# Preparing weights twice instead of storing them: a Strassen-type FNet and GEGLU kernel on one core

## The chip, the core and the metric

The kernel runs on one core of a Trainium2 chip. The metric is the device time of the whole program in microseconds (us). The engines are TensorE (PE: matmuls; PEld: its weight loads), VectorE (DVE), ScalarE (ACT), GpSimd (POOL) and SyncE (SP, which here only issues transfers).

## The reference

```
xn = layernorm(x)                                   # x: 2048 x 448
a, b = xn @ hid_re.T, xn @ hid_im.T
s = seq_re @ a - seq_im @ b                         # 2048 x 2048 matrices
g = silu((gelu(xn @ w_gate) * (xn @ w_up)) @ w_down) # 448 -> 1792 -> 448
out = x + s * g
```

## The kernel before

All matmuls take float32r operands, and a number is held as a high and a low part, so that one product of two blocks is three matmuls (`three`: high by high, high by low, low by high); a fourth, half-empty k-block is stacked so that it needs two (`two`). "Splitting" a tile is an ACT copy into the high part and a DVE subtract for the low part (`split`, L126).

The 2048 rows are four column tiles c = 0 to 3 of 512 (the columns of the transposed, normalised input: `xth`, `xtl`). The 1792 hidden features are 14 tiles f of 128. The tiles f = 0 and 1 are multiplied plainly. For f = 2 to 13 a block (`strassen`, L419) handles two columns c and e = c + 1 at once with seven-product sums of Strassen's kind. The second loop (L858) goes through these blocks twice: run p = 0 with columns 0 and 1, run p = 1 with columns 2 and 3, 24 blocks in all, numbered n. Everything is scheduled by hand: each engine does its instructions in the order of the program.

**A block.** PE makes x1, x2, x3, x4 in PSUM banks, later adds further products onto x1, x3 and x4, and where `q` is absent also makes an x5. ACT copies x1 to m; DVE forms u, m, c21 from the banks; ACT takes the gelu; DVE multiplies; the result is split into an `hs` tile (six of these in turn, `hs_tile`, L345). The second column's multiplication and split are left for the next block (`late`). Between the products PE does row tiles (`send`, `down_one`, L376): six matmuls of 448 columns that multiply hs by the prepared wd, added by DVE (for f = 0 and 1 copied by ACT) into `gacc`. Up to four are sent in a block, at dn[0] to dn[3]; their list dq grows by eight after every odd f. `preps` (before: one call, after the gelu of x1) holds the preparation of the next block's weights. DVE operations of the block in the profile: L443, L450, L455, L477, L478, L485, L491, L498, L503, and L394 for gacc.

**PSUM banks.** x1 to x5 take turns in banks 0 to 3 (`mm_tile`), row tiles in 6 and 7 (`o_tile`), and for later groups also in 4 and 5.

**Weights of a block.** `load_s` (L261) fetches ten raw 128x128 blocks of f into `raw` (512 KB at L265, 128 KB at L266). `sums_s` (L277) makes the Strassen sums in place, on POOL in the loop (L281 to L285). `split_s` (L287) then copies 15 blocks to the high part in one ACT operation (L290, 128x1920) and subtracts on DVE (L291, 128x1408; L292, 64x512 for the stacked blocks). The prepared weights lie in one of two slots; the slot of block n + 1 is filled during block n. In the first run they are also stored to device memory (`store_s`, L299: 960 KB and 704 KB), and in the second run they are fetched from there (`fetch_s`, L303), two blocks ahead, in three slots. The same is done with the prepared wd of a pair f, f + 1: `prep_d` (L318, ACT L320, DVE L321), stored at L834, fetched at L909.

**Terms of a run.** Besides the weights a block needs t1 to t4 (sums of the columns' k-blocks 0 and 1, `ts`) and, from some block on, q1 to q4 (the same with k-blocks 2 and 3, `tq`). They are made from the whole columns that lie in device memory as `xw`: transfers into tmp(0) and tmp(1), a DVE subtract, a split. In the first run q is made in `q_step` 0 to 3 (loads L673 to L683): step 0 before the blocks, 1 in f = 3, 2 and 3 in f = 4; q is used from f = 5. For the second run t is made in the last block of the first (`t1_load`, `t1_sums`, `t1_split`), q in its first block (`q_load1`, `q_step1`); q is used from its f = 3.

**Also on the queues.** `sum_step` (L745) copies and accumulates `sums` between places in device memory, used by the last stage: two copies of 896 KB on SP in one block out of three (L756), two accumulating ones on POOL two blocks later (L758). `gsp` keeps gacc of columns 2 and 3 during the first run, `sp` keeps column 1's xth and xtl, whose place holds q of the second run. At the end of the second run the hidden DFT matrices are loaded and split (`e_load`, `e_split`), and the next stage begins (`hid_mm`, L991), in which the last eight row tiles are sent, four behind each of its first two steps.

Of the kernel before, what the change touches and what calls it, by code (L numbers as in the profile page):

```python
# [8 lines left out]
F32 = mybir.dt.float32  # L9
# [4 lines left out]
P = 128  # L14
# [33 lines left out]
def fnet_geglu(ctx: ExitStack, tc: tile.TileContext, x, ca, ct, cp, et, wgu, wss, wd, out):  # L48
# [60 lines left out]
    turns = {"mm": 0, "tp": 0, "o": 0, "all": 0}  # L109

    def in_turn(kind, name):

        first, n = {"mm": (0, 4), "tp": (4, 2), "o": (6, 2), "all": (0, 8)}[kind]
        turns[kind] += 1
        return bank(first + turns[kind] % n, name)
# [152 lines left out]
    NAMES = ("s1", "s2", "s3", "s4", "s4q", "a11", "a12", "a22", "k2g", "k2u", "s2q")  # L268
# [8 lines left out]
    def sums_s(eng):  # L277


        r = raw_s.rearrange("p (b f) -> p b f", b=17)  # L280
        eng.tensor_add(r[:, 1:16:14], r[:, 0:14:13], r[:, 8:17:8])  # L281
        eng.tensor_sub(r[:, 3:15:11], r[:, 6:13:6], r[:, 0:14:13])
        eng.tensor_sub(r[:, 2], r[:, 1], r[:, 6])
        eng.tensor_sub(r[:64, 11], r[:64, 15], r[:64, 12])
        eng.tensor_sub(r[:, 4:6], r[:, 7:10:2], r[:, 2:12:9])  # L285

    def split_s(slot):  # L287
        h, l = slot
        src = raw_s[:, P:]
        nc.scalar.activation(h, src[:, :WH], AF.Copy)  # L290
        nc.vector.tensor_sub(l, src[:, :WL], h[:, :WL])  # L291
        nc.vector.tensor_sub(h[64:, WL:], src[64:, WL:WH], h[64:, WL:].bitcast(F32))  # L292
        return parts_of(slot)


    w_at = {f: dram.tile([P, WH + WL], F32, name=f"wp{f}") for f in range(2, NF)}
    d_at = {g: dram.tile([P, 4 * D], F32, name=f"dp{g}") for g in range(1, len(GROUPS))}

    def store_s(f, slot):  # L299
        nc.sync.dma_start(w_at[f][:, :WH], slot[0].bitcast(F32))  # L300
        nc.sync.dma_start(w_at[f][:, WH:], slot[1].bitcast(F32))

    def fetch_s(f, slot):  # L303
        nc.sync.dma_start(slot[0].bitcast(F32), w_at[f][:, :WH])
        nc.sync.dma_start(slot[1].bitcast(F32), w_at[f][:, WH:])
        return parts_of(slot)
# [11 lines left out]
    def prep_d(grp, rv, late=False):  # L318
        w = d_view(grp[0] // 2)
        nc.scalar.activation(w[:, 0], rv, AF.Copy)  # L320
        low = lambda: nc.vector.tensor_sub(w[:, 1], rv, w[:, 0])  # L321
        if late:
            return w, low
        low()
        return w
# [17 lines left out]
    hs_of, hs_n = {}, [0]  # L343

    def hs_tile():  # L345
        i = hs_n[0] % 6
        hs_n[0] += 1
        return a_h[i // 3][:, 1024 * (i % 3) :][:, :1024].rearrange("p (a b) -> p a b", a=2)

    def new_hs(f, c):  # L350
        hs_of[f, c] = hs_tile()
# [23 lines left out]

    def down_one(gi, c, wdn, kk):  # L376
        if gi > 0 and kk >= 2:
            po = tp_tile(f"po{gi}_{c}_{kk}")
        else:
            po = o_tile(f"po{gi}_{c}_{kk}")  # L380
        n = 0
        for i, f in enumerate(GROUPS[gi]):
            hs = hs_of[f, c]
            for a, b in ((0, 0), (0, 1), (1, 0)):
# [4 lines left out]
                n += 1  # L389
        ga = gacc[c][:, kk]  # L390
# [28 lines left out]
    def strassen(f, p, w, q, late, dn, preps):  # L419
# [8 lines left out]
        def bank(i):  # L428
            return mm_tile(f"x{i}_{f}_{p}")
# [3 lines left out]
        x1 = bank(1)  # L433
# [5 lines left out]
        x2 = bank(2)  # L439
# [6 lines left out]
        x3 = bank(3)  # L446
# [3 lines left out]
        nc.vector.tensor_add(m, u, x3)  # L450
        x4 = bank(4)
# [3 lines left out]
        nc.vector.tensor_add(m, m, x4)  # L455
# [6 lines left out]
        if f in GROUPS[1] and p == 0:  # L462
            preps()
            dn[1]()
        else:
            dn[1]()
            preps()
# [5 lines left out]
        if q:  # L473
            three(x3, w["k2u"], q[4])
        else:
            other(x3, w, 1, c)
# [31 lines left out]
    with tc.manual_schedule():  # L508
# [7 lines left out]
        junk = hs_tile()[:, 0]  # L516
# [98 lines left out]
        wdn, d_low = prep_d(GROUPS[0], draw, True)  # L615
# [52 lines left out]

        T = 1, 2, 4, 3

        def q_load(i):

            if i == 0:  # L673
                nc.sync.dma_start(tmp(0), xw_at(1, 3))
                nc.sync.dma_start(tmp(1), xw_at(0, 3))
            elif i == 1:
                nc.sync.dma_start(tmp(0), xw_at(1, 2))
            elif i == 2:
                nc.sync.dma_start(tmp(1), xw_at(0, 2))
            elif i == 3:  # L680
                nc.sync.dma_start(tmp(0), xw_at(1, 3))
                for r in range(2):
                    nc.sync.dma_start(tmp(1)[64 * r : 64 * r + 64], xw_at(1, 2)[:64])  # L683

        def q_step(i):
            if i == 0:
                tq[0] = eight(sb.tile([P, 4096], FR, name="tq0", tag="u1"))
            a, b = tmp(0), tmp(1)
            if i == 1:
                nc.vector.tensor_sub(a[:64], a[:64], b[:64])  # L690
            else:
                nc.vector.tensor_sub(b, *((a, b), None, (b, a), (b, a))[i])
            split(*tq[0][T[i]], a if i == 1 else b)
            q_load(i + 1)

        w_of = {}


        for c in (2, 3):
# [27 lines left out]
            else:  # L727
                t_split0(1)
                t_split0(2)
                nwdn, low_d = prep_d(GROUPS[1], draw, late=True)  # L730
                between1 = [lambda: t_split0(3), lambda: (t_split0(4), q_step(0))]
            m1, h1, l1 = gateup(1, c, ws[1], between1)
            m1()
            if c == 2:
                q_load(0)
                h1()
                l1()
                w_of[0, 2] = split_s(slots[0])
# [639 lines left out]
```

## Time and profile before

| what | value |
|---|---|
| time, median of three runs | 807.59 us (806.33 to 809.71) |
| profiled execution, its own time | 804.55 us |
| its span, first to last instruction | 802.8 us |
| matmuls | 4052 |
| mean granted TensorE clock | 0.989 |
| bytes moved by transfers | 205.95 MB |

In the views a row `A:B` is a stretch of the span in us: its length, then busy time and number of instructions of PE, PEld, DVE, ACT and POOL, the granted clock, the mean busy share of the 16 DMA engines, and GB/s. In a timeline a row has start, length, engine, line, operation, output and inputs, shapes and count, and in brackets the idle time of the engine before it with what ended it. In a group's row stand the count, the busy time, the mean ns of one, and after the bar the idle time ahead of it. In the list of transfers stand the issuing queue, the count, the size and the median us from issue to landing. In the chain a row has start, length and what the time went to.

### The profile page before, as it was taken

The page shows a single profiled execution, that of the slowest core. Times are in us where ns is not written, and L with a number is a line of the kernel's source. Part 1 is how long each engine was busy: PE and PEld are TensorE (multiplying, and loading weights), DVE is VectorE, ACT ScalarE, POOL GpSimd, SP SyncE. Part 2 cuts the span into 40 slices and gives each one's busy share as a digit, 9 for nine tenths or more (in the row PEclk, how much of TensorE's full clock was granted, in tenths as well). Part 3 has the DMA queues.
Part 4 walks back from the last instruction along what each step waited for, and adds up shares of the span by engine and source line. Part 5 has one row for each costly group of instructions (what it writes and reads, how often), then busy time and mean ns, then how long its engine had stood idle before and what let it go on. Part 6 is the DMA issues. An engine that isn't in the chain of part 4 may idle for free.

```text
span 802.8 us, 11336 instructions
## 1 busy us (share of the span) xinstructions
PE 774.4 (96%) x4052; PEld 691.3 (86%) x4052; DVE 598.2 (75%) x1045; ACT 316.2 (39%) x424; POOL 76.0 (9%) x102
## 2 busy tenths in 40 slices
PE   9999987999996899999999999999999999999997
PEld 7987776887875778888888999999999999999997
DVE  7877857768677575656576576789797977879697
ACT  3765333433233222212133475554444444444441
POOL 2002222412320000000000000000000000000000
PEclk9999998999999899999999999999999999999999
DMA  8476894999979999858852281396978979696985
GB/s 308 83 222 207 328 299 157 347 298 380 302 264 291 395 328 341 279 227 261 318 131 105 111 352 75 115 318 201 340 221 281 272 264 316 213 342 201 326 266 176
DMA packets 81928, 205.95 MB, mean 257 GB/s; under 512 B 8400, under 2 KB 58448, under 8 KB 80208
## 3 DMA queue, kind: packets, MB, share of 16 engines
q1 hardware_dynamic: 76256, 177.65, 61.4%
q0 software_dynamic: 5472, 27.46, 15.9%
q8 instruction: 32, 0.52, 0.3%
q14 instruction: 24, 0.20, 0.1%
q10 hardware_dynamic: 144, 0.11, 0.0%
HBM read 155.25 MB, written 79.30 MB: 292 GB/s over the span
## 4 chain that ended last, share of the span: by engine, by line
PE 79%; DMA 8%; DVE 6%; ACT 3%; POOL 2%; issue 2%; SPq 0%; DVEq 0%; POOLq 0%; ACTq 0%
PE p L1175 20%; PE x L405 16%; PE po L385 13%; PE p L1178 10%; PE ab L991 9%; PE x L417 3%; DMA w<-wp 3%; PE gu L335 2%; DMA raw<-wss 2%; PE py L1195 1%; PE py L1197 1%; PE py L1196 1%; DMA tmp<-xw 1%; ACT w L290 1%; PE gu L546 1%
## 5 line engine op out<-in xcount | busy, mean ns | idle before, releaser
L385 PE MATMUL po<-wd,hs 128*128 128x448 f32 x672 | 153.8, 367 | 1.8 <-ACT gacc L392 1.4
L385 PEld LDWEIGHTS po<-wd,hs 128*128 128x128 f32 x672 | 126.0, 188 | 17.8 <-ACT gacc L392 2.3
L405 PE MATMUL x<-xt,w 128*128 128x512 f32 x450 | 121.5, 395 | 10.7 <-DMA w<-wp 8.5
L405 PEld LDWEIGHTS x<-xt,w 128*128 128x128 f32 x450 | 85.0, 189 | 28.9 <-issue 8.4
L405 PE MATMUL x<-t,w 128*128 128x512 f32 x276 | 83.4, 404 | 8.3 <-DVE tmp L491 7.1
L394 DVE TENSOR_TENSOR gacc<-gacc,po 128x448 f32<-128x448 f32 x96 | 58.7, 616 | 36.0 <-PE po L385 35.8
L127 ACT ACTIVATE w<-raw 128x896 fp32r<-128x896 f32 (+1 forms) x60 | 54.6, 911 | 61.3 <-DVE raw L1081 31.6
L405 PEld LDWEIGHTS x<-t,w 128*128 128x128 f32 x276 | 53.1, 194 | 19.6 <-DVE tmp L491 7.9
L991 PE MATMUL ab<-w,xt 128*128 128x448 f32 x256 | 68.0, 365 | 0.0
L1175 PE MATMUL p<-xt,w 128*128 128x448 f32 x168 | 54.3, 374 | 0.0
L991 PEld LDWEIGHTS ab<-w,xt 128*128 128x128 f32 x256 | 48.1, 188 | 3.8
L480 ACT ACTIVATE hs<-tmp 128x512 fp32r<-128x512 f32 x24 | 15.2, 633 | 86.6 <-DVE tmp L478 86.6
L461 ACT ACTIVATE tmp<-x 128x512 f32<-128x512 f32 x24 | 14.4, 598 | 88.3 <-PE x L405 79.4
L127 ACT ACTIVATE w<-f 128x896 fp32r<-128x896 f32 (+1 forms) x34 | 30.2, 889 | 42.7 <-DVE f L1081 18.9
L128 DVE TENSOR_TENSOR w<-raw,w 128x896 fp32r<-128x896 f32 (+1 forms) x41 | 42.8, 1047 | 4.3 <-ACT w L127 3.8
L1220 POOL DMA_DIRECT2D cc<-x x14 | 12.4, 882 | 289.3 <-DVE raw L1080 107.4
L417 PE MATMUL x<-xt,w 128*128 128x512 f32 x116 | 37.0, 399 | 1.1 <-ACT xt L127 0.5
L1175 PE MATMUL p<-ts_g,w 128*128 128x448 f32 x112 | 36.4, 374 | 0.0
L1175 PE MATMUL p<-ts_u,ts_tmp 128*128 128x448 f32 x112 | 36.3, 374 | 0.0
L1175 PE MATMUL p<-hs,w 128*128 128x448 f32 x112 | 35.6, 374 | 0.0
L1080 DVE TENSOR_TENSOR raw<-raw 128x128 f32<-128x128 f32 x69 | 19.8, 287 | 20.8 <-DMA raw<-sums 20.4
L991 PE MATMUL ab<-wd,xt 128*128 128x448 f32 x96 | 35.1, 365 | 0.0
(273 smaller groups left out, 1700.5 us busy)
## 6 DMA issues: line engine op xcount, KB each, us to landing
sums<-ca SPq DMA_DIRECT2D x16, 896.0 KB, 11.0
sums<-ca POOLq DMA_DIRECT2D x16, 896.0 KB, 11.4
raw<-ct SPq DMA_DIRECT2D x69, 192.0 KB, 4.4
wp<-w SPq DMA_DIRECT2D x12, 960.0 KB, 7.3
w<-wp SPq DMA_DIRECT2D x12, 960.0 KB, 9.5
ts_u<-td SPq DMA_DIRECT2D x24, 448.0 KB, 6.0
ts_g<-td SPq DMA_DIRECT2D x24, 448.0 KB, 6.5
raw<-sums SPq DMA_DIRECT2D x69, 128.0 KB, 4.4
```

The source lines that it names most:

```text
L127: nc.scalar.activation(h, src, AF.Copy)
L128: nc.vector.tensor_sub(l, src, h)
L335: nc.tensor.matmul(ps[:, cols], a, xt[:, k, cols], start=n == 0, stop=n == len(mm) - 1)
L385: nc.tensor.matmul(po[:, :D], hs[:, a, kk * P : (kk + 1) * P], wdn[:, b, i], start=n == 0, stop=n == 5,)
L394: nc.vector.tensor_add(ga, ga, po[:, :D])
L405: nc.tensor.matmul(ps, a[i], b[j], start=first and n == 0, stop=n == 2, skip_group_check=True)
L417: nc.tensor.matmul(ps, a[0], x_, start=False, stop=True, skip_group_check=True)
L480: nc.scalar.activation(hs[:, 0], g1, AF.Copy)
L991: nc.tensor.matmul(p[:, :D], a, b, start=n == 0, stop=n == len(mm) - 1)
L1080: nc.vector.tensor_add(s2, cr1, s1)
L1175: nc.tensor.matmul(ps[q][:, :D], h, v, start=u % UN == 0, stop=False, skip_group_check=True)
L1178: nc.tensor.matmul(ps[q][:, :HD], l, v[:, :HD], start=False, stop=u % UN == NS - 1, skip_group_check=True,)
```

## The change

- **Weights prepared anew.** `store_s`, `fetch_s` and the two stores in device memory (`wp`, `dp`) are removed. Blocks of both runs load the raw weights, sum them on POOL and split them; the wd of each pair is loaded and split in both runs. Slots alternate by n; the last block has a third slot.
- **Preparation dealt out.** The order of the raw blocks is changed so that the seven plain ones lie together. `split_s` gives three parts, and a block has three places for them: the plain blocks ahead of x3, then POOL's sums; the high parts of the sums after x4; the low parts where preparation stood, followed by the next raw load.
- **The terms, one step a block.** `t_load` and `t_step` replace the routines for q and t: subtract, high and low part at the three places, the low part followed by the loads of the next step. First run: q in f = 2, 3 and 4 (step 0's subtract before them, the rest of it and step 1 in f = 2); t of the second run in f = 6 to 9; its q in f = 10, 11, 12 and in the second run's f = 2. `sp` is stored at f = 9 instead of 8.
- **Banks.** x1 to x4 have banks 0 to 3, x5 has 2, and the product that was added onto x3 has a bank of its own, 4 (x6). Row tiles take turns in 5, 6 and 7.
- **Row tiles a step later.** In f = 2 two are sent and in f = 3 two (before one and three), in f = 4 three, and in the second run's f = 12 six instead of five; in the next stage three behind each of the first three steps. An hs tile is given back to a list when its last row tile is sent.
- **DFT matrices.** One is split in f = 12 and three in f = 13, instead of two and two.

```diff
-    turns = {"mm": 0, "tp": 0, "o": 0, "all": 0}
+    turns = {"mm": 0, "tp": 0, "o": 0, "x": 0, "po": 0, "all": 0}
...
     def split_s(slot):
...
-        nc.scalar.activation(h, src[:, :WH], AF.Copy)
-        nc.vector.tensor_sub(l, src[:, :WL], h[:, :WL])
-        nc.vector.tensor_sub(h[64:, WL:], src[64:, WL:WH], h[64:, WL:].bitcast(F32))
-        return parts_of(slot)
+        n = 6 * P
+        def plain():
+            nc.scalar.activation(h[:, n : n + 7 * P], src[:, n : n + 7 * P], AF.Copy)
+            nc.vector.tensor_sub(l[:, n:], src[:, n:WL], h[:, n:WL])
+        def high():
+            nc.scalar.activation(h[:, :n], src[:, :n], AF.Copy)
+            nc.scalar.activation(h[:, WH - 2 * P :], src[:, WH - 2 * P : WH], AF.Copy)
+        def low():
+            nc.vector.tensor_sub(l[:, :n], src[:, :n], h[:, :n])
+            nc.vector.tensor_sub(h[64:, WL:], src[64:, WL:WH], h[64:, WL:].bitcast(F32))
+        return plain, high, low
-    def store_s(f, slot):
-    def fetch_s(f, slot):
...
     def strassen(f, p, w, q, late, dn, preps):
+        def x_tile(i):
+            return bank((0, 1, 2, 3, 2, 4)[i - 1], f"x{i}_{f}_{p}")
...
         dn[0]()
+        preps[0]()
-        x3 = bank(3)
+        x3 = x_tile(3)
         three(x3, w["s3"], t3, True)
...
-        nc.vector.tensor_add(m, u, x3)
+        nc.vector.tensor_add(c21, u, x3)
...
-        nc.vector.tensor_add(m, m, x4)
+        nc.vector.tensor_add(m, c21, x4)
+        preps[1]()
...
             dn[1]()
-            preps()
+            preps[2]()
+        x6 = x_tile(6)
+        three(x6, w["a22"], t4, True)
...
         if not q:
-            x5 = bank(5)
+            x5 = x_tile(5)
             other(x5, w, 1, e, True)
-            nc.vector.tensor_add(m, m, x5)
-        three(x3, w["a22"], t4)
...
-        nc.vector.tensor_add(c21, u, x3)
+        nc.vector.tensor_add(c21, c21, x6)
         nc.vector.tensor_mul(g1, g1, c21)
...
+        if not q:
+            nc.vector.tensor_add(m, m, x5)
...
+        def t_load(i, p, k1, k2):
+            c, e = 2 * p, 2 * p + 1
+            for n, v in ({0: (e, k1), 1: (c, k1)}, {0: (e, k2)}, {1: (c, k2)}, {0: (e, k1)}, {})[i].items():
+                nc.sync.dma_start(tmp(n), xw_at(*v))
...
+        def t_step(i, places, p, k1, k2):
...
+            return sub, high, low
...
+        def weights(n):
+            if n == len(blocks):
+                return [], [], []
+            slot = slots[2 if n == len(blocks) - 1 else n % 2]
+            w_of[blocks[n]] = parts_of(slot)
+            plain, high, low = split_s(slot)
+            next_ = [lambda: load_s(blocks[n + 1][1])] if n + 1 < len(blocks) else []
+            return [plain, lambda: sums_s(nc.gpsimd)], [high], [low, *next_]
...
+        for n, (p, f) in enumerate(blocks):
             g = f // 2
             dn, q = [send] * 4, tq[p]
+            prep = weights(n + 1)
+            step = []
+            if f % 2 == 0 and n:
+                d_raw[0] = load_d(GROUPS[g])
+            if f % 2 and 1 < n < len(blocks) - 1 or n == len(blocks) - 2:
+                prep[1].append(lambda: weights_d(g))
+                prep[2].append(lambda: low_of[g]())
             if p == 0:
                 if f == 2:
+                    prep[0][:0] = q_steps[0][1:]
+                    prep[2].append(q_steps[1][0])
+                    dn = [nop, send, q_steps[1][1], then(send, q_steps[1][2])]
                     nc.sync.dma_start(gsp[0], gacc[2].rearrange("p k d -> p (k d)"))
                 elif f == 3:
+                    dn = [nop, send, send, low_d]
                 elif f == 4:
+                    dn[0] = nop
...
+                if 2 < f < 5:
+                    step = [q_steps[f - 1]]
+                elif 6 <= f < 12:
+                    step = [t1_steps[f - 6]]
+                elif f == 12:
+                    step = [t1_steps[6][:1]]
+                if f == 9:
                     nc.sync.dma_start(sp, a_x[1].bitcast(F32))
+            elif f == 2:
+                q = None
+                for v, w in zip(prep, (*t1_steps[6][1:], t1_steps[7][0])):
+                    v.append(w)
+                dn[2:] = [then(send, v) for v in t1_steps[7][1:]]
...
+            elif f == NF - 3:
+                e_load(2)
+            elif f == NF - 2:
+                dn[1] = dn[3] = then(send, send)
+                prep[2].append(lambda: e_split(2))
+                prep[2].extend([lambda b=b: e_load(b) for b in (1, 0, 3)])
+            elif f == NF - 1:
+                prep[2].extend([lambda b=b: e_split(b) for b in (1, 0, 3)])
+                dn = [then(send, send), send, nop, nop]
+            if step:
+                for v, w in zip(prep, step[0]):
+                    v.append(w)
+            prep = [then(*v) for v in prep]
             late = strassen(f, p, w_of[p, f], q, late, dn, prep)
...
+            elif p == 0 and f == 5:
+                t_load(0, 1, 0, 1)
+            elif p == 0 and f == 9:
+                t_load(0, 1, 3, 2)
             sum_step(n)
...
-            if k < 2:
-                for _ in range(4):
+            if k < 3:
+                for _ in range(3):
                     send()
```

More of the change, by code (lines that the diff above doesn't have):

```diff
@@ L374, in gateup @@
         return act(f, c, pg)
+    sends = [False]
     def down_one(gi, c, wdn, kk):
[L377 to L380, printed above, removed]
+        po = in_turn("po" if sends[0] else "o", f"po{gi}_{c}_{kk}")
         n = 0
@@ L389, in down_one @@
                 n += 1
+        if kk == 3:
+            hs_free.extend(hs_at.pop((f, c)) for f in GROUPS[gi])
         ga = gacc[c][:, kk]
@@ L438, in strassen @@
         late[0]()
-        x2 = bank(2)
+        x2 = x_tile(2)
         three(x2, w["s2"], t2, True)
@@ L871, in fnet_geglu @@
                 elif f == 4:
+                    dn[0] = nop
+                if f < 5:
                     q = None
[L873 to L882 removed]
```

236 lines of the change are left out of this document (75 added, 161 removed).

## The prediction

> **What bounds the kernel now.** I read the page first, for the shares and the chain of work that ended last.
>
> ```profile
> span 802.8 us, 11336 instructions
> PE 774.4 (96%) x4052; PEld 691.3 (86%) x4052; DVE 598.2 (75%) x1045; ACT 316.2 (39%) x424; POOL 76.0 (9%) x102
> PE 79%; DMA 8%; DVE 6%; ACT 3%; POOL 2%; issue 2%; SPq 0%; DVEq 0%; POOLq 0%; ACTq 0%
> ```
>
> PE is the bound, and the change leaves it the same matmuls. So nothing can be won but time in which PE waits or runs at a lower clock. A tenth of the chain, DMA and POOL, is not PE's. To find where, I cut the part that the change touches (72.19 to 431.85 us) at the starts of the blocks, as PE's timeline shows them. The two runs through the columns have twelve blocks each, f = 2 to 13; the first row below is f = 2 of the first run, the tenth is f = 2 of the second.
>
> ```profile
> core 0: us, PE busy (x) PEld busy (x) DVE busy (x) ACT busy (x) POOL busy (x), PEclk, DMA share, GB/s
> 72.19:84.49 12.30, 11.11 (x48) 8.66 (x47) 8.90 (x12) 4.96 (x7) 2.40 (x3) 1.00 0.61 237
> 84.49:99.06 14.57, 13.56 (x60) 10.92 (x59) 11.85 (x16) 5.82 (x8) 4.08 (x5) 1.00 0.99 360
> 99.06:114.03 14.97, 14.54 (x66) 12.12 (x65) 11.27 (x17) 6.07 (x9) 5.55 (x7) 1.00 1.03 334
> 114.03:137.46 23.43, 16.37 (x64) 13.48 (x63) 13.29 (x19) 6.15 (x8) 4.07 (x5) 0.85 0.53 157
> 137.46:178.78 41.32, 41.32 (x190) 35.49 (x189) 30.52 (x45) 14.99 (x19) 11.81 (x17) 1.00 0.96 317
> 178.78:208.70 29.92, 28.71 (x127) 23.35 (x126) 25.27 (x36) 10.32 (x13) 8.55 (x12) 1.00 1.00 371
> 208.70:222.48 13.78, 13.78 (x64) 11.64 (x62) 6.76 (x11) 4.00 (x6) 3.01 (x5) 1.00 0.87 255
> 222.48:240.47 17.99, 16.15 (x64) 12.99 (x64) 15.52 (x21) 6.32 (x8) 3.92 (x5) 0.91 0.76 284
> 240.47:254.24 13.77, 13.77 (x64) 11.64 (x62) 11.02 (x18) 5.09 (x8) 1.65 (x2) 1.00 1.03 281
> 254.24:279.09 24.85, 16.32 (x67) 13.30 (x67) 15.05 (x26) 5.75 (x10) 0.00 (x0) 0.86 1.02 371
> 279.09:294.13 15.04, 14.33 (x64) 11.75 (x63) 11.88 (x20) 4.51 (x9) 1.64 (x2) 1.00 1.02 364
> 294.13:431.85 137.72, 137.72 (x632) 118.30 (x630) 84.19 (x132) 32.66 (x54) 4.93 (x6) 1.00 0.74 242
> ```
>
> The last row is ten blocks with PE busy throughout, so an undisturbed block takes 13.77 us. It holds 39 products of 512 columns and four row tiles (24 matmuls of 448). Next, what PE waited for where a block took longer.
>
> ```profile
> 74.75 2.07 PE L405 MATMUL x<-t,w 128*128 128x512 f32 x6 [1.05 <-ACT tmp L360]
> 97.74 1.49 PE L385 MATMUL po<-wd,hs 128*128 128x448 f32 x6 [0.96 <-ACT gacc L392]
> 124.98 1.65 PE L405 MATMUL x<-t,w 128*128 128x512 f32 x3 [7.06 <-DVE tmp L491]
> 223.33 0.73 PE L405 MATMUL x<-xt,w 128*128 128x512 f32 x2 [0.69 <-ACT w L290]
> 224.99 0.50 PE L405 MATMUL x<-xt,w 128*128 128x512 f32 x1 [0.93 <-DVE w L291]
> 228.00 1.32 PE L405 MATMUL x<-tq,w 128*128 128x512 f32 x3
> 229.16 1.40 PE L385 MATMUL po<-wd,hs 128*128 128x448 f32 x6
> 262.47 1.19 PE L405 MATMUL x<-xt,w 128*128 128x512 f32 x2 [8.06 <-DMA w<-wp]
> 421.82 2.60 PE L385 MATMUL po<-wd,hs 128*128 128x448 f32 x12
> 424.25 0.86 PE L405 MATMUL x<-t,w 128*128 128x512 f32 x3
> ```
>
> Twelve row-tile matmuls take 424.25 - 421.82 = 2.43 us, 0.2025 each, a row tile 1.215; so a product takes (13.77 - 24 x 0.2025) / 39 = 0.2285. The fourth view, the chain in order of time, says what stood behind the waits.
>
> ```profile
> 110.19 10.91 DMA tmp<-xw
> ...
> 207.73 10.45 DMA raw<-wss
> ...
> 240.88 23.21 DMA w<-wp
> ```
>
> All three are transfers that landed late and were issued in stretches whose DMA share stood near 1. The wait at 124.98 is named after DVE, but DVE itself was standing behind the first of these, the rows for q_step(3). The one at 262.47 is the fetch of the stored weights for the second run's first block.
>
> **What can be had.** Blocks f = 2, 3, 4 of the first run and f = 2 of the second have 41 products instead of 39 (0.46 more), and the first run's f = 2 and 3 send one and three row tiles instead of four. Ideal and lost, in us: f2 13.77 + 0.46 - 3.65 = 10.58, lost 1.72; f3 13.01, lost 1.56; f4 14.23, lost 0.74; f5 9.66; f6 to f8 nothing; f9 and f10 2.38; f11 nothing; f12 4.22; f13 nothing; second run f2 24.85 - 14.23 = 10.62; f3 1.27; the rest nothing. The sum is 32.2 us: 20.3 in the first run, 11.9 in the second. The row tiles are only dealt out differently (43 and 49 instead of 44 and 48 before the next stage), so the ideal stays. No edit can win more than this in these blocks, and the change touches the later stage only in how eight remaining row tiles are spread.
>
> **The change part by part.** First the transfers.
>
> ```profile
> wp<-w SPq DMA_DIRECT2D x12, 960.0 KB, 7.3
> w<-wp SPq DMA_DIRECT2D x12, 960.0 KB, 9.5
> raw<-wss SPq DMA_DIRECT2D x12, 512.0 KB, 5.7
> ...
> DMA to landing us min/median/max: 3.4/5.7/10.7
> ```
>
> The last line is for the 512 KB loads of raw weights (L265). Storing the prepared weights (960 KB and 704 KB a block) and fetching them again goes, as do the stores and fetches of the prepared wd (896 KB a pair of blocks). By the sizes in the code the first run moves 640 (raw) + 1664 + 224 + 448 + 1195 (four sums of 896 KB in three blocks) = 4171 KB a block now, which is the 317 GB/s and 0.96 share of the row from 137.46. After, it is 640 + 224 + 1195 and up to 512 for the row tiles of t1 and q: 2570 KB at most, a share near 0.6. The second run goes from 1664 + 448 + 1195 = 3307 to about 2060 KB.
>
> So the fetch ahead of the second run (10.6 us lost) has nothing in its place: its first block's weights are prepared in the block before, as all others. The raw loads that were late in f9, f10 and f12 (2.4 + 4.2) have less in front of them. The rows for q's last step are asked for in f3 and used in f4, a good half block later, no longer within f4; of f5's 9.7 most should go. The two waits for gacc copies in f3 and f4 came from two banks; now three take turns, and the 1920-wide ACT copy is in three pieces.
>
> What is added to the engines: twelve more preparations, in the second run. Prices:
>
> ```profile
> L291 DVE TENSOR_TENSOR w<-raw,w 128x1408 fp32r<-128x1408 f32 x11 | 17.9, 1625 | 19.5 <-ACT w L290 19.5
> L292 DVE TENSOR_TENSOR w<-raw,w 64x512 fp32r<-64x512 f32 x11 | 7.6, 690 | 0.3
> L321 DVE TENSOR_TENSOR wd<-raw,wd 128x896 fp32r<-128x896 f32 x6 | 6.5, 1090 | 0.1
> L128 DVE TENSOR_TENSOR tq<-tmp,tq 128x512 fp32r<-128x512 f32 x4 | 3.0, 761 | 2.8 <-ACT tq L127 2.8
> L498 DVE TENSOR_TENSOR tmp<-tmp 128x512 f32<-128x512 f32 x11 | 8.5, 773 | 2.2 <-ACT tmp L494 2.2
> ...
> L498 DVE TENSOR_TENSOR tmp<-tmp 128x512 f32<-128x512 f32 x8 | 5.5, 686 | 0.0
> L290 ACT ACTIVATE w<-raw 128x1920 fp32r<-128x1920 f32 x7 | 12.6, 1805 | 9.7 <-POOL raw L285 9.7
> ```
>
> DVE does (84.19 - 2 x 1.09) / 10 = 8.2 us a block in the second run (the two are splits for the next stage). Weights add 1.63 + 0.69 and about 0.16 for cutting one subtract in two (an estimate: between 64x512 and 128x1408 a column costs 1.04 ns, which leaves 0.16 fixed): 10.7, and 11.8 where a wd is prepared. In the first run f6 to f11 take t1's and q's steps on top, a subtract and a split of 0.69 to 0.76: 12.2, and 13.3 with a wd. All stay under 13.77, the last by only 0.5. ACT's extra 1.8 and a wd copy every second block, and POOL's 3.0 (row from 208.70), are far from a limit. So DVE still hides behind PE, though a heavy block makes it some 2.5 us late: it stands idle until the second row tile, then has the low parts, the wd and the step ahead of its next PSUM read. PE bears that: bank 4 is wanted a block later, and the sum that frees x4 is done before this queue. If that cover goes, PE pays the excess.
>
> PSUM: the last gate-up pair lies in banks 1 and 2, so x2 of f2 waits for the gelu on bank 1 as x3 does now; ACT is freer there since q's first split moved behind. Between nothing and the 1.05 of now: I take 0.8. A separate bank for x6 takes the place of adding onto x3 and costs no DVE operation: three before and three after.
>
> New waits on in-order engines: DVE and ACT now stand behind row tiles of xw in f2 to f4; behind them on DVE are the sum that frees bank 2 for x5 and the one that frees x4. The cost lies between a gain and the 9.66 of f5; a transfer asked for half a block ahead at a share of 0.6 is nearer to none: 1.2. In the second run's f2, step 7 waits for rows asked for behind 1.8 MB of gacc, and x3 of f3 needs its result: between 0 and the 10.62 of now, nearest to the 1.27 that the same place cost in f3: 0.8. Three splits for the next stage instead of two fall in the last block, the last one after the next stage has begun: 0 to 1.09, I take 0.5. Late weights elsewhere: 0.2. Together 3.5.
>
> On SP's queue the two stores stood between a raw load and the sums of that block. They are gone, but the row-tile loads stand there instead, each waiting for DVE's low part of a step, and the sums wait behind them; in f2 this sends the first sums some 3 us later. POOL's accumulations wait for those sums and for the new sums_s ahead of them on POOL; the sums are used in the last stage only, so this costs nothing unless they block a raw load, which the third rival prices.
>
> How much such remnants cost depends on the clock. In f12 the waits were 0.69 + 0.93 and a few tenths, but the block lost 4.22, since PE ran at (229.16 - 228.00) / 3 = 0.39 us a product for some time after. By that row 3.5 us of waits could cost 8. The Trainium skill (TensorE: Matmul & The Clock Gate, Part 1) has the clock halve after an idle window of about 3.4 us; by that rule waits this short cost only themselves and the sum stays. f12 speaks against it, so both ends are kept.
>
> **Sum.** The profiled execution took 804.55 us, 1.75 more than its span, against a median of 807.59 (806.33 to 809.71) of three runs, 1.0038 of it. 804.55 - 32.2 + 3.5 = 775.9; on the scale of the median 778.8 us.
>
> **Rivals.** *The waits move along.* The in-order DVE and ACT stand behind the row tiles as long as PE did: f5's 9.66 returns in full, and half of the second run's 10.62, less the 2.0 counted: 775.9 + 13.0 = 788.9, 792 by the median. For it: q's last rows have 1.8 MB of sums and a weight load ahead of them. Against: the share.
>
> *DVE and POOL exclude each other.* L498 takes 773 ns in the first run, where POOL works, and 686 in the second. If a sum on POOL held DVE for its whole length, 3.0 us would be added to a block: in f6 to f11 12.75 + 3.0 - 13.77 = 2.0, twelve in all, and in the second run 11.25 + 3.0 - 13.77 = 0.5, six: 794 us, 797 by the median. Against: in f6 to f8 POOL works and PE loses nothing. The Trainium skill (SBUF — State Buffer, Who interferes with whom) states such an exclusive lock for a DVE operation with two SBUF inputs; the 87 ns show it as occasional.
>
> *Slower: the raw load becomes a chain through all blocks.* It is issued when DVE has the low parts, about 11 us into a block; the next block's ACT copy, DVE subtract, the sums behind it and then x4's second half (11.1 us in) hang on it with about 3.5 us of work, as do POOL's sums and the next weights. So it must land within about 10.3 us; each us beyond is lost in 22 blocks. It decides at 10.3, and is slower than before from 11.8. At 12.5: 776 + 48 = 824, 827 by the median. For it: 10.7 was seen, and 10.45 in the chain. Against: the median of 5.7, under a heavier load.
>
> **How the numbers follow.** Forecast 0.73, moved waits 0.13, exclusion 0.04, slower chain 0.05, and 0.05 that something unseen eats the gain (0.04 to no change, 0.01 to slower). About 0.5% (4 us) is what a measurement of this kernel can tell from no change. Faster 0.90; same 0.04; slower 0.06. The range starts at 773, the ideal by the median (775.3) less the spread of runs, and ends at 793, with the doubled remnants (784) and the first rival in it.
>
> **What would show it.** Right: no w<-wp or dp rows, PE busy all through 254 to 270, blocks of 13.77 us, DVE about 11 us a block in the second run, the part from 72 us to the next stage near 331 us instead of 359.7. Wrong: PE waiting for DVE w or ACT w in many blocks (third rival); blocks of 14 to 16 us with DVE full (second); a PE gap of several us in f3 to f5, or in f2 and f3 of the second run, with DVE behind tmp<-xw (first).

## The result, and the profile after

The changed kernel takes 778.82 us (median of six runs, 776.04 to 780.49) against 807.70 us (six runs, 806.33 to 809.71). The ratio is 0.9636, with a 95% interval of 0.9611 to 0.9661. The forecast was 778.8.

The profiled execution of the changed kernel is the longest of its six: 780.49 us, with a span of 778.7. From its page, the busy time of the engines, the transfers, and the chain by engine:

```profile
span 778.7 us, 11499 instructions
...
PE 766.2 (98%) x4052; PEld 687.8 (88%) x4052; DVE 639.2 (82%) x1099; ACT 347.1 (45%) x490; POOL 126.4 (16%) x162
...
DMA packets 80634, 165.46 MB, mean 212 GB/s; under 512 B 8000, under 2 KB 62656, under 8 KB 78912
...
PE 61%; DVE 15%; DMA 14%; issue 3%; ACT 3%; POOL 2%; SPq 1%; DVEq 0%; POOLq 0%
```

PE does the same 4052 matmuls and is now busy for 98% of the span instead of 96%. DVE has 41 us more to do and POOL 50 us more; 40.5 MB fewer are moved. That the chain's share of PE fell from 79% to 61% says little, I think: once nearly every block is full, a chain traced backwards can run through work that ended just in time.

The same part as before, cut at the starts of the blocks. The first four rows are f = 2 to 5 of the first run, the fifth is f = 6 to 10, then f11, f12 and f13; the ninth and tenth are f = 2 and 3 of the second run, then its other ten blocks, and the last row is the next stage.

```profile
core 0: us, PE busy (x) PEld busy (x) DVE busy (x) ACT busy (x) POOL busy (x), PEclk, DMA share, GB/s
72.14:84.44 12.30, 12.03 (x54) 9.87 (x53) 11.03 (x16) 6.21 (x11) 3.42 (x6) 1.00 0.41 99
84.44:96.22 11.78, 11.78 (x54) 9.95 (x53) 11.31 (x16) 6.51 (x12) 3.55 (x4) 1.00 0.56 210
96.22:109.22 13.00, 13.00 (x60) 11.07 (x59) 12.63 (x18) 5.33 (x9) 6.96 (x7) 1.00 0.84 224
109.22:123.00 13.78, 13.78 (x65) 11.83 (x63) 9.92 (x15) 5.24 (x9) 3.59 (x5) 1.00 0.43 109
123.00:191.86 68.86, 68.86 (x316) 59.15 (x315) 63.61 (x94) 28.83 (x47) 23.38 (x29) 1.00 0.70 214
191.86:209.46 17.60, 14.21 (x64) 11.56 (x62) 11.07 (x17) 6.33 (x10) 3.41 (x5) 1.00 0.56 138
209.46:223.46 14.00, 14.00 (x63) 11.86 (x64) 13.29 (x20) 4.75 (x8) 3.68 (x5) 1.00 0.67 229
223.46:237.24 13.78, 13.78 (x65) 11.83 (x64) 12.97 (x19) 5.70 (x9) 5.52 (x7) 1.00 0.55 117
237.24:252.16 14.92, 14.49 (x66) 12.12 (x65) 10.33 (x17) 5.50 (x9) 3.93 (x5) 1.00 0.91 293
252.16:267.60 15.44, 14.05 (x64) 11.75 (x63) 14.97 (x22) 6.11 (x10) 3.77 (x5) 1.00 0.51 176
267.60:406.53 138.93, 138.93 (x637) 119.44 (x636) 113.73 (x167) 55.45 (x87) 41.11 (x53) 1.00 0.60 165
406.53:778.70 372.17, 367.16 (x2161) 345.40 (x2159) 297.62 (x551) 169.56 (x198) 14.54 (x18) 1.00 0.73 242
```

Read it by the lengths: f = 5 to 10 and f13 are at 13.77 to 13.78 us, and f = 3 and 4 at their own ideal (11.8 and 13.0 for fewer row tiles). Five blocks are not: f2 (0.5 over its ideal of 11.80), f11 (3.8), f12 (0.2), and f2 and f3 of the second run (0.7 and 1.7), 6.9 us in all where there were 32.2. The granted clock is 1.00 in every row. The part from 72 us to the next stage took 406.53 - 72.14 = 334.4 us instead of 359.7 (near 331 was foretold). The next stage took 372.17, 1.2 more than before (370.95).

PE's timeline at the waits that are left:

```profile
73.93 1.66 PE L403 MATMUL x<-t,w 128*128 128x512 f32 x6 [0.27 <-DVE tmp L359]
...
205.61 1.66 PE L403 MATMUL x<-xt,w 128*128 128x512 f32 x6 [2.40 <-DVE tmp L454]
...
209.46 0.98 PE L403 MATMUL x<-xt,w 128*128 128x512 f32 x3 [0.99 <-ACT tmp L461]
...
246.66 0.96 PE L403 MATMUL x<-xt,w 128*128 128x512 f32 x3 [0.43 <-DVE tmp L449]
...
258.37 0.51 PE L415 MATMUL x<-xt,w 128*128 128x512 f32 x1 [1.39 <-DVE xt L701]
...
407.78 0.67 PE L984 MATMUL ab<-w,xt 128*128 128x448 f32 x2 [0.48 <-DVE w L845]
```

The largest, at 205.61 in f11, is named after DVE. As with the waits of the kernel before, one has to follow it back: the timelines of POOL, SP, ACT and DVE in that stretch.

```profile
187.79 1.66 POOL L776 DMA_DIRECT2D sums<-ca  x2
...
190.47 0.33 SPq L265 DMA_DIRECT2D raw<-wss  x1
...
200.44 0.95 ACT L294 ACTIVATE w<-raw 128x896 fp32r<-128x896 f32 x1 [3.84 <-DMA raw<-wss]
...
201.43 0.83 DVE L295 TENSOR_TENSOR w<-raw,w 128x640 fp32r<-128x640 f32 x1 [3.56 <-ACT w L294]
...
203.39 0.77 DVE L690 TENSOR_TENSOR tmp<-tmp 64x512 f32<-64x512 f32 x1 [1.14 <-DMA tmp<-xw]
...
204.87 0.69 DVE L454 TENSOR_TENSOR tmp<-tmp,x 128x512 f32<-128x512 f32 x1
```

POOL issues the two accumulating transfers of 896 KB at 187.79, SP asks for the raw weights at 190.47, and they are there only at about 200.4: some 10 us. ACT, DVE, the rows for a step of q (`tmp<-xw`) and the sum that frees x4 are late one after the other. The window of that load, and the landing times of all 512 KB loads in this kernel:

```profile
190.47:200.42 9.95, 9.95 (x47) 8.57 (x46) 6.85 (x11) 2.39 (x4) 0.00 (x0) 1.00 0.99 227
```

```profile
DMA to landing us min/median/max: 3.3/3.7/10.0
```

While the load was on its way the mean share of the DMA engines was 0.99. Over the loop this is a pattern. Seven raw loads are asked for while a pair of accumulations is under way, and they take 7.4 to 10.0 us; six of them land 0.2 to 0.7 us behind the pair's second transfer. The others of the loop take 3.3 to 3.8 us, but for one of 6.9 behind the 2 MB store of `sp`.

### The profile page after: what moved, and what is told of

It is laid out like the page before. It is cut to its first block, busy times and chain, and to the rows that moved or that the text cites. A ratio compares the mean times of both kernels' runs of the same rounds, so it can differ in the third digit from the quotient of the medians.

```text
span 778.7 us, 11499 instructions
## 1 busy us (share of the span) xinstructions
PE 766.2 (98%) x4052; PEld 687.8 (88%) x4052; DVE 639.2 (82%) x1099; ACT 347.1 (45%) x490; POOL 126.4 (16%) x162
## 4 chain that ended last, share of the span: by engine, by line
PE 61%; DVE 15%; DMA 14%; issue 3%; ACT 3%; POOL 2%; SPq 1%; DVEq 0%; POOLq 0%
PE p L1168 14%; PE x L403 11%; PE po L381 10%; PE ab L984 9%; PE p L1171 7%; DMA raw<-wss 5%; DMA raw<-sums 4%; PE gu L330 3%; PE x L415 2%; DMA out<-cc 1%; DVE w L128 1%; PE gu L548 1%; DVE w L302 1%; PE py L1188 1%; PE py L1190 1%
## 5 line engine op out<-in xcount | busy, mean ns | idle before, releaser
L403 PE MATMUL x<-xt,w 128*128 128x512 f32 x450 | 119.7, 392 | 3.8 <-DVE tmp L454 2.4
L403 PE MATMUL x<-t,w 128*128 128x512 f32 x276 | 80.0, 392 | 0.3 <-DVE tmp L359 0.3
L281 POOL TENSOR_TENSOR raw<-raw 128x256 f32<-128x256 f32 x23 | 19.3, 840 | 217.6 <-DMA raw<-wss 178.4
L298 ACT ACTIVATE w<-raw 128x768 fp32r<-128x768 f32 x24 | 20.2, 843 | 39.6 <-POOL raw L285 39.6
L415 PE MATMUL x<-xt,w 128*128 128x512 f32 x116 | 36.1, 391 | 1.4 <-DVE xt L701 1.4
```

Source lines behind the costliest of these rows:

```text
L298: nc.scalar.activation(h[:, :n], src[:, :n], AF.Copy)
L403: nc.tensor.matmul(ps, a[i], b[j], start=first and n == 0, stop=n == 2, skip_group_check=True)
L415: nc.tensor.matmul(ps, a[0], x_, start=False, stop=True, skip_group_check=True)
```

## The experiments

Three theories stood at the start. *Transfers*: the waits went because the stores and fetches no longer lie in front of the loads. *Dealing out*: they went because the preparation in three places bears late transfers. And, for the waits that are left, *accumulations*: POOL's transfers hold up the raw load. Each kernel below is the changed kernel with one edit unless it says otherwise; "the changed kernel" is 778.8 us in the first four, 778.3 (the control) after.

**The stores put back.** In the first run the prepared weights are again written to device memory behind the raw load; nothing reads them.

```diff
+        def store_s(f, slot):
+            nc.sync.dma_start(w_at[f][:, :WH], slot[0].bitcast(F32))
+            nc.sync.dma_start(w_at[f][:, WH:], slot[1].bitcast(F32))
...
             next_ = [lambda: load_s(blocks[n + 1][1])] if n + 1 < len(blocks) else []
+            if n < NF - 2:
+                next_.append(lambda: store_s(blocks[n][1], slot))
```

> The changed kernel, with the two stores of each prepared weight (960 and 704 KB) back in the first run, behind the raw load; nothing reads them. Theory (the waits went because the transfers went): the first run's DMA share is back near 1, raw loads and row tiles land late again, PE waits for weights and for steps of q; 10 to 20 us more than the 778.8 of the changed kernel, 789 to 799. Rival (the dealt-out preparation and the banks bear late transfers, the stores cost little by themselves): at most 3 us more, up to 782.

Measured: 799.52 us (796.83 to 801.87), ratio 0.9899 (0.9862 to 0.9936): 20.7 us of the gain are gone. From the timeline of this kernel, PE, SP and DVE:

```profile
155.74 0.42 SPq L819 DMA_DIRECT2D wp<-w  x1
...
156.68 0.42 SPq L677 DMA_DIRECT2D tmp<-xw  x1
...
169.37 0.69 DVE L692 TENSOR_TENSOR tmp<-tmp 128x512 f32<-128x512 f32 x1 [3.71 <-DMA tmp<-xw]
...
171.50 2.93 PE L403 MATMUL x<-xt,w 128*128 128x512 f32 x6 [2.85 <-DVE tmp L454]
...
222.49 2.93 PE L403 MATMUL x<-xt,w 128*128 128x512 f32 x6 [2.87 <-DVE tmp L454]
```

The stores stand ahead of the load of rows (`tmp<-xw`) in SP's queue: asked for at 156.68, the rows are there at 169.3. DVE's in-order stream stands at these rows, and PE stands behind DVE. The raw loads themselves hardly changed (median 4.1 us), and PE waited for no weights: the size is the theory's, just above its 799, but the waits for weights that it expected did not come. The two largest waits, those shown, are in blocks in which a pair of accumulations was under way as well. So the dealing out does not make the kernel proof against these transfers, and taking them away matters. But the price comes by the way of the prediction's first rival, which the kernel before did not have in these blocks: this is not a replay of where the time was lost before.

**Preparation in one piece.** All three parts of the preparation are done at the last of the three places.

```diff
-            prep = [then(*v) for v in prep]
+            prep = [nop, nop, then(*prep[0], *prep[1], *prep[2])]
```

> The changed kernel, with all three parts of the preparation (and of the steps of t and q) at the middle place, as before the change; weights are still prepared anew. Theory (transfers): ACT and DVE have the same work in one burst, PE bears most of it, 0 to 4 us more than 778.8. Rival (the dealing out is what keeps PE fed, above all with twelve more preparations): waits for weights in many blocks, 10 us and more, 789 or above.

Measured: 779.55 us (778.74 to 781.18), ratio 0.9655 (0.9632 to 0.9679). The 0.7 us lie within the spread. The dealing out alone, with all else as it is, cannot be told from no change. Its profile loses time in another place: no wait in f11, but 1.98 us at 255.87, in the second run's f3.

**Two banks for row tiles.**

```diff
-        first, n = {"mm": (0, 4), "tp": (4, 2), "o": (6, 2), "x": (0, 5), "po": (5, 3), "all": (0, 8)}[kind]
+        first, n = {"mm": (0, 4), "tp": (4, 2), "o": (6, 2), "x": (0, 5), "po": (6, 2), "all": (0, 8)}[kind]
```

> The changed kernel, with row tiles taking turns in two banks instead of three (6 and 7; 5 stays empty in the loop). Theory: DVE clears a bank within a row tile or two, so 0 to 2 us more than 778.8, all of it where DVE is about 2.5 us late in the heavy blocks f = 6 to 11. Rival (PE needs the third bank all along): over 0.3 us in each of 24 blocks, 786 and more.

Measured: 784.84 us (782.69 to 786.22), ratio 0.9716 (0.9689 to 0.9743), 6 us more. PE's waits for gacc from there on, with the next stage beginning before the second:

```profile
391.08 1.48 PE L381 MATMUL po<-wd,hs 128*128 128x448 f32 x6 [1.10 <-DVE gacc L392]
...
414.82 2.61 PE L381 MATMUL po<-wd,hs 128*128 128x448 f32 x6 [2.07 <-DVE gacc L392]
...
426.77 1.48 PE L381 MATMUL po<-wd,hs 128*128 128x448 f32 x6 [1.92 <-DVE gacc L392]
```

The third bank earns most where three tiles are sent in a row, which the change itself brought into the next stage. In the loop the waits sum to about 1.8 us, in the next stage to 4.0. The six matmuls at 414.82 take 2.61 us instead of 1.48, as the clock was halved there (0.50), so this wait cost 1.1 us more than itself. Neither expectation held: the loss is three times the theory's 2 us, and it is not spread over the 24 blocks as the rival had it.

**q's steps asked for where they were.** Steps 1 to 3 go back to f = 3 and 4; everything else stays.

```diff
-                    dn = [nop, send, q_steps[1][1], then(send, q_steps[1][2])]
+                    dn = [nop, send, nop, send]
...
+                    prep[2].extend(q_steps[1])
...
+                    prep[2][:0] = q_steps[2]
+                    dn[2] = then(send, *q_steps[3])
```

> The changed kernel, with the steps of q where they were before: step 1 in the middle of f = 3, 2 and 3 within f = 4. Theory (the emptied queue is what counts): the last rows land in 3 to 5 us instead of 10.9 and the wait in f = 5 is 0 to 4 us; 779 to 783. Rival (asking half a block earlier is what counts): the wait in f = 5 is back at 7 us and its remnant of low clock with it, 787 to 789.

Measured: 784.03 us (782.27 to 784.82), ratio 0.9704 (0.9676 to 0.9732), 5.2 us more. The timeline around f5:

```profile
101.13 1.71 POOL L776 DMA_DIRECT2D sums<-ca  x2
...
105.82 1.13 SPq L681 DMA_DIRECT2D tmp<-xw  x2
...
116.72 0.50 PE L415 MATMUL x<-tq,w 128*128 128x512 f32 x1 [3.00 <-ACT tq L697]
...
119.19 1.65 PE L403 MATMUL x<-t,w 128*128 128x512 f32 x3 [1.24 <-DVE tmp L493]
```

The rows asked for at 105.82 were used at 115.3, 9.5 us later, with POOL's accumulations on their way and no stores. PE waited 4.2 us there, where the kernel before lost 9.66. So of f5's loss about half went without the earlier asking, with the transfers that were taken away or with something else of the change. The other half went because the rows are now asked for earlier. Neither theory had it alone. Whether later accumulations would have won the second half too was not tried.

**Control.** The changed kernel again, beside the next three on one chip.

> The changed kernel as it is, as a measure on this chip for the next three. All theories: 776 to 780, as in its six runs, with f = 11 of the first run at 13.8 us in the fast ones and near 17.6 us in the others.

Measured: 778.26 us (775.73 to 779.07), ratio 0.9626 (0.9604 to 0.9648). In its profile the wait in f11 is 1.5 us instead of 2.4: this loss differs from one execution to the next.

**Accumulations later.** POOL issues them behind the first of its five sums of weights, that is, when the raw weights have landed, instead of ahead of the load.

```diff
         eng.tensor_add(r[:, 1:16:14], r[:, 0:14:13], r[:, 9:17:7])
+        if behind_first:
+            behind_first()
...
+            sums_ = lambda: sums_s(nc.gpsimd, lambda: sum_step(n - 1, (2,)))
...
-            sum_step(n)
+            sum_step(n, (0, 2) if n == len(blocks) - 1 else (0,))
```

> The changed kernel, with POOL's two accumulating transfers issued behind the first of a block's five sums instead of behind the last and behind the block, so that they begin at the start of a block and are over when the next raw load is asked for. Theory (the raw loads that take 8 to 12 us instead of 3.3 are those that share the DMA engines with these accumulations): all raw loads land within 3 to 5 us, f = 11 is back at 13.8, the second run's f = 2 and 3 lose 1 us instead of 2.4; 774 to 776.5. Rival (the 2 MB store of sp is what delays f = 11): f = 11 still over 15 us in the profile, no change over 1 us.

Measured: 774.26 us (774.18 to 775.31), ratio 0.9585 (0.9567 to 0.9602), below the control's interval, and its runs spread over 1.1 us where the control's spread over 3.3. The stretch that held f11's gap, by windows, and the largest of PE's waits in the loop of this kernel:

```profile
core 0: us, PE busy (x) PEld busy (x) DVE busy (x) ACT busy (x) POOL busy (x), PEclk, DMA share, GB/s
189.00:206.50 17.50, 17.50 (x82) 15.13 (x81) 16.72 (x24) 7.35 (x13) 4.19 (x5) 1.00 0.46 120
```

```profile
104.36 0.96 PE L405 MATMUL x<-xt,w 128*128 128x512 f32 x3 [0.71 <-DVE tmp L451]
```

In the loop the longest landing of a raw load fell from 10.0 to 5.7 us, and the waits in f11 and in the second run's f2 and f3 are gone. By its median this is the fastest kernel of the study, and it beats both kernels.

**`sp` stored a block earlier.** The 2 MB store of column 1 goes out at f = 8, as before the change.

```diff
-                if f == 9:
+                if f == 8:
                     nc.sync.dma_start(sp, a_x[1].bitcast(F32))
```

> The changed kernel, with sp stored at the start of f = 8 instead of f = 9, ahead of the sums of that block. Theory (accumulations): the raw load of f = 10 lands in 4 us instead of 7, but that of f = 11 still takes 8 to 9; f = 11 loses 0 to 1.5 us instead of 3.8; 776 to 778. Rival (sp): f = 11 at 13.8 us as well, and the median at the lower end of the control, 776.

Measured: 776.16 us (774.49 to 778.42), ratio 0.9603 (0.958 to 0.9627). The wait in f11 is gone from its profile too, as the rival had it. The longest landing is still 10.0 us, but it belongs to a load asked for in f13; the one that f11 hangs on took 7.1 us instead of 9.95. The trace shows why. In the changed kernel the raw load before it stood behind the store of `sp` (6.9 us, here 3.5), so POOL's sums and the accumulations behind them came late, at 187.79 instead of 183.80, and the load of f11 was asked for 2.7 us behind them instead of 6.0. So f11's loss takes both, the accumulations ahead of the load and the store that the change itself had put into f9; either edit removes it from its profile. The interval overlaps the control's, so the 2 us are not settled.

**Both, and the fetch of gacc a block later.** The two edits above, and in the second run the 1.8 MB of gacc asked for in f = 3 instead of f = 2.

```diff
                 dn[2:] = [then(send, v) for v in t1_steps[7][1:]]
+            elif f == 3:
...
                 v = sb.tile([P, 8 * D], F32, name="gacc2", tag="u1")
```

> The changed kernel with three edits: the accumulations behind the first sum, sp stored at f = 8, and gacc of columns 2 and 3 fetched in f = 3 of the second run instead of f = 2, so that the rows of the last step do not stand behind it. Theory: f = 11 at 13.8 and the second run's f = 2 and 3 within 1 us of the ideal; 773.5 to 775.5, below both kernels. Rival: the moved transfers meet others (the sums of the second run's f = 2, a wd load) and give back what they gained; 776 to 779.

Measured: 775.64 us (773.74 to 776.04), ratio 0.9594 (0.9574 to 0.9614). It is no better than the accumulations alone, which had left only 0.3, 0.7 and 0.5 us of waits from the start of the loop on; there was little left for the other two to win.

**The same edit on the kernel before.** POOL's accumulations behind the first sum, in the first run of the kernel before.

```diff
-                sums_s(nc.gpsimd)
+                sums_s(nc.gpsimd, lambda: sum_step(f - 3, (2,)))
```

> The kernel before, with POOL's accumulating transfers behind the first of a block's sums in the first run, as in the sixth experiment. Theory (the stores and fetches of prepared weights fill the DMA engines, the accumulations only add to it): f = 5 and the second run's f = 2 lose as before, 0 to 4 us faster than 807.9. Rival (the accumulations were the cause all along, and the changed kernel merely moved them): 10 us faster or more, below 798.

Measured: 803.53 us (802.62 to 805.45) against 807.97, ratio 0.9941 (0.9911 to 0.9971). Its two large waits are still there:

```profile
125.22 1.65 PE L407 MATMUL x<-t,w 128*128 128x512 f32 x3 [7.70 <-DVE tmp L493]
...
260.80 1.19 PE L407 MATMUL x<-xt,w 128*128 128x512 f32 x2 [8.23 <-DMA w<-wp]
```

So the accumulations were worth about 4.4 us in the kernel before as well (2.3 to 7.2 by the interval), but they were not what made f5 and the second run's start wait.

**Row tiles sent as before.** In f = 2, 3, 4, f = 12 of the second run and the next stage (four behind each of two steps).

```diff
-                    dn = [nop, send, q_steps[1][1], then(send, q_steps[1][2])]
+                    dn = [nop, send, q_steps[1][1], q_steps[1][2]]
...
-            if k < 3:
-                for _ in range(3):
+            if k < 2:
+                for _ in range(4):
```

> The changed kernel, with the row tiles sent as before: one in f = 2, four in f = 4, five in f = 12 and four behind each of the next stage's first two steps. Theory (the later sending only keeps a row tile from waiting for the hs tile made just before): 0 to 3 us more than the changed kernel's 778.5, in waits for ACT hs or DVE hs at the head of an even block. Rival (the four at a time are too many for three banks in the next stage, as two banks were for three): 3 us and more, in waits for DVE gacc behind its first two steps.

Measured: 780.38 us (777.86 to 782.92), ratio 0.9654 (0.9626 to 0.9682). Its profile has two waits in the next stage that the changed kernel lacks:

```profile
413.03 1.47 PE L381 MATMUL po<-wd,hs 128*128 128x448 f32 x6 [0.85 <-DVE gacc L392]
...
423.36 1.50 PE L381 MATMUL po<-wd,hs 128*128 128x448 f32 x6 [0.74 <-DVE gacc L392]
```

They sum to 1.6 us, about what the median rose by: within the theory's 3 us, but in the place that the rival named. The interval overlaps the control's, so the size is not settled.

## Why the prediction was right, step by step

**The ideal and what could be had.** The blocks do run at 13.77 to 13.78 us, and on the scale of the profiled execution the 32.2 us held as a limit: the kernel with the later accumulations has a span of 772.4 against 802.8 - 32.2 = 770.6. Of the 32.2, all but 6.9 came back in the profiled execution of the changed kernel. By the median the limit did not hold: 774.26 lies below the 775.3 that the prediction took for the ideal. The profiled execution of the kernel before (804.55) was shorter than all six timed ones (806.33 and more), so an ordinary one probably lost more than 32.2.

**The transfers.** There are no wp or dp rows any more. The share in f6 to f10 is 0.70, where near 0.6 was worked out; raw loads land in a median of 3.7 us instead of 5.7. The stores put back in the queue cost 20.7 us. f5's 9.66 is wholly gone, and with q's steps at their old places about half of it came back; the prediction counted on the emptier queue and on the earlier asking without dividing them.

**The added work hides.** In f6 to f10 DVE is busy for 63.61 of 68.86 us, 12.7 a block, between the 12.2 and 13.3 that were worked out, and PE loses nothing. In the second run's ten steady blocks, less three splits of 1.09, it has (113.73 - 3.27) / 10 = 11.0 us a block, as told. The prediction had PE busy all through 254 to 270 us, and that did not hold: the 1.39 at 258.37 lies there.

**The rest, predicted 3.5.** f2 lost 0.5 (0.8 was taken), but not as told: x2 found its bank free, and the wait of 0.27 at 73.93 is that of x3 for bank 2, until DVE's multiply by the up product (L359) had read it. q's rows in f2 to f4: nothing (1.2). The third split at the start of the next stage: 0.48 (0.5). The second run's f2 and f3: 2.4 (0.8); in f3 the mechanism is as told, with DVE's L701 as the releaser, but it is dearer, and it went when the accumulations were moved. "Late weights elsewhere", 0.2, is the term that was mis-sized: f11 and f12 lost 4.1 in the profiled execution. The prediction let the accumulations cost nothing "unless they block a raw load". They did, and moving them won 4.0 us. f11 also needed the store of `sp` in f9, to which the prediction gave no price. The sum of the rest in the profile is thus 6.9 + 0.5 = 7.4, and the next stage took another 0.7 us that no wait in its records accounts for; what that is stays open. It differs between executions: from its first matmul on the stage took 372.8 us in the control and 371.6 in the kernel with the later accumulations.

**Why the number agrees nonetheless.** The sum was 775.9 on the scale of a profiled execution and was raised by 1.0038 to the median. The profiled execution of the changed kernel took 780.49, which is 4.6 more; but it lies above its own median, where that of the kernel before lay below. Median against median, 28.8 us were forecast and 28.9 measured. That closeness is partly luck: the profiled run, at 780.49, has f11's loss in full, and the other runs, down to 776.04, left no timeline that shows how much of it they had.

**The rivals.** Moved waits: in the changed kernel only the 1.39 of the second run's f3, but the stores put back produce just this, with DVE at tmp<-xw. DVE and POOL: in the second run's ten steady blocks POOL now works, and u * m there (the group of L500, which was L498) reads

```profile
L500 DVE TENSOR_TENSOR tmp<-tmp 128x512 f32<-128x512 f32 x10 | 8.1, 813 | 1.5 <-ACT tmp L496 1.5
```

against 686 ns before: dearer by 127 ns an operation, and PE still loses nothing. The Trainium skill (SBUF — State Buffer, Who interferes with whom) states an exclusive lock for such operations. The row agrees that DVE is held up, but the mean hides how: five of the ten ran beside POOL's sums and took 795 to 1109 ns, the other five 684 to 693, one of these beside POOL too. A delayed one lost 0.1 to 0.4 us, less than most sums on POOL take (0.46 to 1.02 by their means). The raw load as a chain: landings of 7.4 to 7.7 us cost nothing in the second run's ten steady blocks, one of 8.9 cost f5 nothing, and one of about 10 us, with late rows for q behind it, cost f11 3.8. So the mechanism is there, and 10.3 was somewhat high for its threshold; but it struck hard in one block and not in 22. Two of the prediction's figures are slightly off by its own numbers: this rival is slower than before from 10.3 + 28.7 / 22 = 11.6, not 11.8, and the doubled remnants give 783, not 784.

**The clock.** The doubled remnants did not come: at 205.61 six products after a wait of 2.40 us take 1.66 us, as at 73.93 after 0.27, and the clock of f11 is 1.00. With the stores put back, waits little longer were followed by a halved clock; windows of that kernel from the ends of two of its waits:

```profile
core 0: us, PE busy (x) PEld busy (x) DVE busy (x) ACT busy (x) POOL busy (x), PEclk, DMA share, GB/s
171.50:174.50 3.00, 3.00 (x7) 2.42 (x8) 2.94 (x5) 0.00 (x0) 0.00 (x0) 0.51 0.01 3
222.40:225.40 3.00, 2.91 (x7) 2.33 (x8) 2.94 (x5) 0.00 (x0) 0.00 (x0) 0.50 0.00 0
```

There 2.85 and 2.87 us of waiting cost about another 1.3 us each (six products in 2.93 instead of 1.66). The Trainium skill (TensorE: Matmul & The Clock Gate, Part 1) gives an idle window of about 3.4 us that runs freely, not from the start of a gap. The 2.40 us agree with it; that 2.85 us are enough is not what a single gap measured against 3.4 would give, and no run here shows where such a window begins. Nor does the length of the wait alone decide: after 2.07 us with two banks for row tiles (414.82) the clock was 0.50 over the next 3 us, and after 1.92 at 426.77 it was 1.00. In the kernels of this case, single waits of 1.98, 2.07, 2.14, 2.51, 2.85 and 2.87 us were followed by half the clock within six matmuls, and those of 1.65, 1.92 and 2.40 were not.

**What stays open.** How the 25 us divide between fewer bytes and the changed order was tried for f5 and, by the stores, for the first run. For the second run's start it was not tried apart: without the stored weights there is no fetch to wait for. The bank of its own for x6 was not tried apart either. Whether 774.3 and 775.6 (the accumulations alone, and all three edits) differ at all is not settled either.

## What to carry to other kernels

When a result is cheap to make again on engines that have room, storing it and fetching it can cost the bound engine more through the loads that queue behind it than through its own transfer: count per block what lies ahead of the one load that everything hangs on. Follow a wait past the engine it is named after, and then look at all queues, a background queue on another engine too, at the moment at which the late load was asked for. A transfer that nobody waits for is best issued when the urgent load has landed, not ahead of it.

## What the runs showed of the hardware

Two accumulating transfers of 896 KB on POOL's queue took a 512 KB load on SP's queue from 3.3 to 3.8 us to 7.4 to 10.0, most often until just behind the second of them. The mean DMA share over f11, where it did most harm, was only 0.56, but 0.99 while the load was on its way. A mean share over a block is therefore no bound on the landing of one load within it. And the length of a wait of PE did not tell what came after it: 2.07 us were followed by half the clock over the next 3 us, 2.40 us by the full clock.
